# An operand shifted by 32 bytes and five steps reordered in a fused convolution and two-layer kernel

## The chip, the core and the metric

The kernel runs on one core of a Trainium2 chip. The metric is the device time of one execution in microseconds (us). A profile records one execution, instruction by instruction, on the engines PE (matrix products; its weight loads are listed as PEld), DVE (vector), ACT (activations, copies), POOL (a second elementwise engine, which also issues some DMAs) and SP (issues most of the DMAs).

## The reference

The input x has 8 sequences of 4096 tokens with 192 channels. A causal convolution of 7 taps per channel (the weights are a softmax over the taps, one set for each of 8 heads) gives y. Two dense layers follow:

```python
y   = sum over k of w[head, k] * x_padded[:, t + k, :]      # (8, 4096, 192)
h   = y.reshape(32768, 192) @ w_in                           # 192 -> 2048
g   = h * clip(h + 3, 0, 6) / 6
out = g @ w_out                                              # 2048 -> 192, float32
```

## The kernel before

The tokens are worked off in 32 blocks of 1024. Block 0 is a special case (its convolution, the rounding of the weights and a plain second layer stand there together). Blocks 1 to 31 each run `first_layer` (lines 457 to 515) and `second_layer` (lines 548 to 812).

**Convolution.** The tile `x` holds the 192 channels as 64 partitions times 3 thirds, with the lower 512 tokens of the block in partitions 0 to 63 and the upper 512 in partitions 64 to 127. `conv_jobs` (line 922) returns seven jobs that build the tile `y`: one ACT multiplication (tap 0, line 924) and six DVE operations (taps 1 to 6, line 926, one instruction each). There is one buffer for `x`: the load of the next but one block (`load_x`, lines 88 and 89, two DMAs on SP's queue) cannot start until tap 6 has read the old one. The loop at lines 1023 to 1038 spreads the jobs: taps 0, 1 and 2 of block i+2 stand in the list `between` of `second_layer(i)`, taps 3 to 6 in the list `jobs` of the following first layer, where key -1 is ahead of the first unit and key n is behind unit n.

**Splitting.** y is split for a product in several passes: `split_high` (ACT, line 420) writes a high part, `split_rest` (DVE, line 423) the low part, both into `y_own`, two tiles of the pool `yo`. `swap_parts` (line 427) copies both parts with the two halves of the partitions exchanged into `y_other`, by four DMAs of SP's queue (lines 299 and 300).

**First layer.** Sixteen units; units 0 to 7 read `y_own` and units 8 to 15 read `y_other`. A unit is 18 matmuls of 64 rows (line 437, three passes by three thirds by two partition halves, the two halves side by side in the array), then `relu` on ACT (line 311) and `gate` on DVE (line 315), which writes g. A unit holds two PSUM banks, one of four slots; the slot is free again after its gate. The last slots of the first layer are the first ones of the second layer.

**Second layer.** g is used as a two by two matrix of blocks A11, A21, A12, A22, and multiplied by w_out in seven products with sums of the blocks: S1 = A21 + A22 (written over A21), S2 = S1 - A11 (over A11), S3 = A11 - A21 in the tile `s3`, later S3 holds S4 = A12 - S2. Products 1, 4 and 5 are cut once more in the same way into seven small ones; their sums are `s1` (POOL, line 534), `s5` (DVE, line 534) and, for A22, the tile `z` and two tiles z2 and z4. z2 and z4 are called `z_early` and lie in the same memory as `y_own`, which is free by then. They are made by ACT (`seed`, line 477) and then by adding DMAs on POOL's queue (`onto`, line 480), in this order: two into `z`, one into the lower half of S1 (line 511), one into z2 (line 512), and one into z4 out of z2 (line 515).

The products of the second layer stand in four streams, one for each 32 columns of the PE array. Every instruction has a due time t in steps of one matmul of 256 columns; `put` appends matmuls, `do(t, ...)` puts a step of another engine at t - 0.5, and lines 806 to 808 emit everything sorted by t. The due time only sets the order in which each engine meets its instructions; when one runs is up to the semaphores. In the later part of the layer stand, by due time, S4's first half (line 760, DVE), `split_rest` (57.3), `swap_parts` (58), tap 0 (60), the add that the code builds for step 3 of product 5 (line 721, reads the bank slice B; due 61), U3's add (line 762, reads the bank `b` between products 6 and 3, due 61), S4's second half (line 763) and the stores.

Two bookkeeping tiles matter for addresses only: `mx` (line 257) and `sm` (line 264), each one float per partition.

Of the kernel before, what the change touches and what calls it, by code (L numbers as in the profile page):

```python
# [11 lines left out]
F32 = mybir.dt.float32  # L12
# [19 lines left out]
def kernel(  # L32
# [9 lines left out]
    P = nc.NUM_PARTITIONS  # L42
# [24 lines left out]
    cst = ctx.enter_context(tc.tile_pool(name="cst", bufs=1))  # L67
    xs = ctx.enter_context(tc.tile_pool(name="xs", bufs=1))
    ys = ctx.enter_context(tc.tile_pool(name="ys", bufs=1))
    yo = ctx.enter_context(tc.tile_pool(name="yo", bufs=1))  # L70
    ot = ctx.enter_context(tc.tile_pool(name="ot", bufs=1))
# [11 lines left out]
    def load_x(i, dma=nc.sync):  # L83
        x = xs.tile([P, K3, PAD + N], F32, name="x")
        head, lower, upper = x_source(i)
        if head:
            nc.vector.memset(x[0:D2, :, 0:PAD], 0.0)
        dma.dma_start(out=x[0:D2, :, head:], in_=lower)
        dma.dma_start(out=x[D2:P, :, :], in_=upper)
        return x  # L90
# [23 lines left out]
    make_identity(nc, ident[:])  # L114
    diag = cnv.tile([P, KC, P], F32, name="diag", bufs=1)
    g = cst.tile([P, NP, 2, G, N], F32, name="g")
    zeros = g[:, 0, 0, 0]
    nc.vector.memset(zeros, 0.0)

# [2 lines left out]
    def own_tiles(name):  # L122
        return [yo.tile([P, K3, N], F32, name=f"{name}{n}", tag=f"y{n}") for n in range(2)]

    y_own, z_early = own_tiles("y"), []
    y_other = cst.tile([P, 2, K3, N], F32, name="y_other")
    w_out = cst.tile([P, NP, 7, DH], F32, name="w_out")
# [126 lines left out]
        if n == 0:  # L254
            load_x0(1, nc.sync, nc.sync)

    mx = cst.tile([P, 1], F32, name="mx")
    nc.vector.tensor_reduce(out=mx[:], in_=w_sb[:], axis=AX.X, op=ALU.max)
    e_sb = cst.tile([P, KC], F32, name="e_sb")
    nc.vector.tensor_tensor(  # L260
        out=e_sb[:], in0=w_sb[:], in1=mx[:].to_broadcast([P, KC]), op=ALU.subtract
    )
    nc.scalar.activation(e_sb[:], e_sb[:], ACT.Exp)
    sm = cst.tile([P, 1], F32, name="sm")
    c_sb = cst.tile([P, KC], F32, name="c_sb")
    half = cst.tile([P, 1], F32, name="half")
    nc.vector.memset(half[:], 0.5)
# [42 lines left out]
    def relu(r6, h):  # L310
        nc.scalar.activation(r6, h, ACT.Relu, bias=half[:], scale=1.0 / 6.0)  # L311

    def gate(g_, h):

        nc.vector.scalar_tensor_tensor(  # L315
            out=g_, in0=g_, scalar=1.0, in1=h, op0=ALU.min, op1=ALU.mult
        )
# [57 lines left out]
    def g_sums(engine, which, slots, width):  # L375

        forms = {
            3: (S3, A11, A21, ALU.subtract),
            2: (S2, S1, A11, ALU.subtract), 4: (S3, A12, S2, ALU.subtract),
        }  # L380
        for n in which:
            o, a, b, op = forms[n]
            for p in slots[::width]:
                r = slice(p, p + width)
                engine.tensor_tensor(out=o[:, r], in0=a[:, r], in1=b[:, r], op=op)  # L385
# [18 lines left out]
    def add(out, x, y, op=ALU.add):  # L404
        nc.vector.tensor_tensor(out=out, in0=x, in1=y, op=op)  # L405
# [9 lines left out]
    m = slice(0, DH)  # L415
# [15 lines left out]
    def products(n, slot, s, steps=range(3), begin=False, end=False):  # L431
        group, c = divmod(n, NP)
        for m_ in steps:
            wn, yn = PASSES[m_]
            for k in range(2):
                r = slice(k * D2, (k + 1) * D2)
                nc.tensor.matmul(  # L437
                    out=psum[:, 2 * slot + k], lhsT=r32(w_in_parts[wn][r, c, s]),
                    rhs=r32(y_other[r, yn, s] if group else y_own[yn][r, s]),
                    start=begin and m_ == 0, stop=end and m_ == 2, skip_group_check=True,  # L440
                )

    def places(n, slot):
        group, c = divmod(n, NP)
        return g4[:, c, 1:3] if group else g4[:, c, 0::3], psum[:, 2 * slot : 2 * slot + 2]


    def sums_a22():

        z2, z4 = (  # L450
            part[:].rearrange("p s n -> p (s n)")[:, : NP * TH // 2]
            .rearrange("p (u t) -> p u t", t=TH)
            for part in z_early
        )
        return z[:, :, 1], z2, z[:, :, 0], z4

    def first_layer(i, jobs):

        def unit(n):
            slot = free_slots.pop(0)  # L460
            for m_ in range(3):
                for s in range(K3):
                    products(n, slot, s, (m_,), s == 0, s == K3 - 1)
            to, both = places(n, slot)
            relu(to, both)
            gate(to, both)
            free_slots.append(slot)

        count = 2 * NP
        x11, x12, x21, x22 = four_parts(A22)  # L470

        def begin_sums():
            z_early[:] = own_tiles("z")
            seed(sums_a22()[1], x11, -1.0)

        def seed(to, x, sign):
            nc.scalar.mul(to, x, sign)  # L477

        def onto(to, x):
            nc.gpsimd.dma_start(out=to, in_=x, accum_op=ALU.add)  # L480


        def z13(u0, u1):
            onto(z[:, u0:u1].rearrange("p u c t -> p (u c) t"), A22[:, 2 * u0 : 2 * u1, halves[1]])

        hu = NP // 4
        s4_sums = {
            hu + 1: [lambda: seed(z[:, :hu, 0], x11[:, :hu], -1.0)],
            hu + 2: [lambda: seed(z[:, :hu, 1], x21[:, :hu], 1.0), lambda: z13(0, hu)],
            NP - 1: [lambda: seed(z[:, hu:, 0], x11[:, hu:], -1.0)],  # L490
            NP: [lambda: seed(z[:, hu:, 1], x21[:, hu:], 1.0), lambda: z13(hu, 2 * hu)],
            NP + 1: [begin_sums],
            NP + 2: [lambda: seed(sums_a22()[3], x12, -1.0)],
        }
        for job in jobs.get(-1, ()):
            job()
        for n in range(count):
            unit(n)
            for job in jobs.get(n, ()):
                job()  # L500
            for job in s4_sums.get(n, ()):
                job()
            if n == 1:
                s1.append(ot.tile([P, NP, N], F32, name="s1", tag="shared")[:])
            if n < NP and n % 2:
                small_sums(s1[-1], A11, (1, 2, 3, 4), nc.gpsimd, every[n - 1 : n + 1])
            if n > NP and n % 2:
                pair = slice(n - NP - 1, n - NP + 1)
                g_sums(nc.gpsimd if n + 1 < count else nc.vector, (3,), range(NP)[pair], 2)
                if n == NP + 3:  # L510
                    onto(S1[:, : NP // 2], A22[:, : NP // 2])
                    onto(sums_a22()[1], z[:, :, 1])
        for pair in (slice(NP - 2, NP), slice(NP - 4, NP - 2)):
            add(S1[:, pair], A21[:, pair], A22[:, pair])
        onto(sums_a22()[3], sums_a22()[1])
# [4 lines left out]
    def four_parts(x):  # L520
        return [x[:, c::2, t] for t in halves for c in range(2)]

    def small_sums(to, x, which, engine=nc.gpsimd, r=every):

        r = slice(r[0], r[-1] + 1)
        x11, x12, x21, x22 = four_parts(x[:, r])
        s1, s2, s3, s4 = four_parts(to[:, r])
        forms = {
            1: (s1, x21, x22, ALU.add), 2: (s2, s1, x11, ALU.subtract),
            3: (s3, x11, x21, ALU.subtract), 4: (s4, x12, s2, ALU.subtract),  # L530
        }
        for n in which:
            o, p, q, op = forms[n]
            engine.tensor_tensor(out=o, in0=p, in1=q, op=op)  # L534
# [13 lines left out]
    def second_layer(i, between):  # L548
        last = i + 1 == NB
        ours = [free_slots.pop(0) for _ in range(3)]  # L550
        d, e, b, c, a, x_ = (psum[:, 2 * n + k] for n in ours for k in range(2))
# [3 lines left out]
        m = slice(0, DH)  # L555
# [3 lines left out]
        late = {}  # L559
# [8 lines left out]
        def do(t, fn, *args, **kw):  # L568
            streams[3].append((t - 0.5, lambda: fn(*args, **kw)))  # L569
# [189 lines left out]
        do(44, sum_s5, 4)  # L759
        do(44, g_sums, nc.vector, (4,), every[:4], 4)  # L760
        do(53, lambda: copy(out=late["p7"], in_=c[m]))
        do(61, lambda: add(late["u3"], b[m], late["p7"]))
        do(61, g_sums, nc.vector, (4,), every[4:], 4)
        do(65.5, lambda: add(late["p7"], late["u3"], p4[:]))
        do(65.5, lambda: store(i, late["p7"], 1, 0))
# [69 lines left out]
    with tc.manual_schedule():  # L835
# [19 lines left out]
        b, b1 = (2 * free_slots[-1] + k for k in range(2))  # L855
# [81 lines left out]
        for r in range(2 * NP):  # L937
# [12 lines left out]
            n = joins.get(r)  # L950
# [42 lines left out]
        conv = []  # L993
# [27 lines left out]
        z = last.tile([P, NP // 2, 2, TH], F32, name="z")  # L1021
        left = []
        for i in range(1, NB):
            jobs = {4 * n + 1: [job] for n, job in enumerate(conv[4:])}
            jobs[-1] = left + conv[3:4]
            first_layer(i, jobs)
            conv = []

            def begin_conv():
                x_tiles[i + 2] = load_x(i + 2)  # L1030
                conv.extend(conv_jobs(i + 2))

            between = []
            if i + 1 < NB:
                between = [(43.6, split_high), (57.3, split_rest), (58, swap_parts)]
            if i + 2 < NB:
                between += [(20, begin_conv), (60, lambda: conv[0]()), (72, lambda: conv[1]()), (73, lambda: conv[2]())]
            left = second_layer(i, between)


# [31 lines left out]
```

## Time and profile before

| what | value |
|---|---|
| time, median of 3 runs | 2243.15 us (2242.98 to 2243.4) |
| the profiled execution | 2243.17 us, span 2241.4 us |
| PE busy | 2227.6 us (99% of the span) |
| DVE, ACT, POOL busy | 1833.1, 1163.6, 900.7 us |
| one first layer (144 matmuls on y_own, 144 on y_other) | about 33.3 us |
| one second layer | 35.36 us in nearly every other block, mostly 35.7 to 36.4 us in those between |
| DMA traffic | 208.1 MB, of which 98.7 MB on POOL's queue |

In the page's groups a line gives line, engine, operation, tiles, partitions by elements and count, then busy time and mean ns of one, then the idle time of the engine ahead of them. Matmuls of line 437 overlap in pairs, so that the time from start to start says more than the mean of one. In a timeline the first column is the start from the beginning of the span, the second the length, and in brackets stands how long the engine had been idle and for what.

### The profile page before, as it was taken

The numbers are of one execution on the slowest core, as the hardware profiler recorded it, in microseconds if no ns is written. First come the engines' busy times: TensorE is split into PE (matmuls) and PEld (weight loads), VectorE is DVE, ScalarE is ACT, GpSimd is POOL, SyncE is SP. The second block draws the span as 40 slices with busy tenths as digits, with TensorE's granted clock in tenths as the row PEclk, the third lists the DMA queues.
The fourth block names the chain that finished last, engine by engine and source line by source line (L and its number), as shares of the span: only waits on it lengthen the run. The fifth ranks groups of instructions, "written<-read, shape, count | busy, mean of one in ns | idle before, by whom it ended". The sixth has DMA issues, their size and how long they took to land.

```text
span 2241.4 us, 51884 instructions
## 1 busy us (share of the span) xinstructions
PE 2227.6 (99%) x22466; PEld 1531.3 (68%) x22466; DVE 1833.1 (82%) x1650; ACT 1163.6 (52%) x1607; POOL 900.7 (40%) x803
## 2 busy tenths in 40 slices
PE   9999999999999999999999999999999999999998
PEld 5567676677666676766767667676667676676766
DVE  8887888878888778887788887788877888878876
ACT  7455554455554555544555445555455554555544
POOL 4534442244432444323444224443244432344423
PEclk9999999999999999999999999999999999999999
DMA  7355544555545545445554455554554544555353
GB/s 163 67 106 91 100 84 83 105 96 89 97 73 102 105 83 103 80 87 107 93 97 83 86 105 94 92 94 74 104 103 83 104 74 93 107 85 99 71 90 63
DMA packets 302181, 208.10 MB, mean 93 GB/s; under 512 B 208608, under 2 KB 261344, under 8 KB 301952
## 3 DMA queue, kind: packets, MB, share of 16 engines
q0 software_dynamic: 70320, 98.65, 28.0%
q1 hardware_dynamic: 230392, 105.86, 22.9%
q8 instruction: 176, 2.88, 0.6%
q10 hardware_dynamic: 1240, 0.27, 0.1%
q14 instruction: 53, 0.43, 0.1%
HBM read 31.72 MB, written 25.17 MB: 25 GB/s over the span
## 4 chain that ended last, share of the span: by engine, by line
PE 83%; DVE 10%; DMA 6%; POOL 1%; issue 0%; ACT 0%; SPq 0%; DVEq 0%; POOLq 0%; ACTq 0%
PE psum L437 45%; PE psum L572 35%; DMA z<-z 5%; DVE s L385 3%; DVE y L423 2%; DVE results L405 2%; PE psum L326 2%; DVE z L405 2%; POOL s L534 1%; PE psum L850 0%; POOL s L385 0%; DVE y L926 0%; DMA w_sb<-in_weight_dram 0%; DMA y_other<-y 0%; POOL z L480 0%
## 5 line engine op out<-in xcount | busy, mean ns | idle before, releaser
L572 PE MATMUL psum<-g,w_out 128*32 128x512 f32 (+1 forms) x6092 | 1051.2, 531 | 0.0
L315 DVE SCALAR_TENSOR_TENSOR g<-g,psum 128x1024 f32<-128x1024 f32 x512 | 618.9, 1218 | 192.5 <-ACT g L311 190.0
L311 ACT ACTIVATE g<-psum,half 128x1024 f32<-128x1024 f32 x512 | 571.4, 1116 | 355.0 <-PE psum L437 350.4
L534 POOL TENSOR_TENSOR s<-g 128x256 f32<-128x256 f32 x248 | 251.6, 1014 | 1005.4 <-DVE g L315 972.2
L572 PE MATMUL psum<-s,w_out 128*32 128x256 f32 (+1 forms) x3272 | 628.9, 571 | 2.9
L437 PE MATMUL psum<-y,w_in 64*128 64x512 f32 x4608 | 548.9, 393 | 0.3
L437 PE MATMUL psum<-y_other,w_in 64*128 64x512 f32 x4608 | 530.1, 386 | 0.1
L572 PEld LDWEIGHTS psum<-g,w_out 128*32 128x32 f32 x6092 | 421.7, 110 | 146.9 <-issue 44.0
L437 PEld LDWEIGHTS psum<-y,w_in 64*128 64x128 f32 x4608 | 428.0, 184 | 135.5 <-issue 26.7
L437 PEld LDWEIGHTS psum<-y_other,w_in 64*128 64x128 f32 x4608 | 431.7, 184 | 92.7 <-DMA y_other<-y 0.5
L926 DVE SCALAR_TENSOR_TENSOR y<-x,c_sb,y 128x1536 f32<-128x1536 f32 x186 | 336.7, 1810 | 2.9 <-ACT y L924 1.8
L572 PE MATMUL psum<-g,w_s 128*32 128x256 f32 x1488 | 322.3, 379 | 0.0
L385 POOL TENSOR_TENSOR s<-g 128x1024 f32<-128x1024 f32 x93 | 301.1, 3238 | 6.5 <-DVE g L315 6.5
L572 PEld LDWEIGHTS psum<-s,w_out 128*32 128x32 f32 x3272 | 180.4, 110 | 168.6 <-issue 116.7
L534 DVE TENSOR_TENSOR g<-g 128x1024 f32<-128x1024 f32 x93 | 111.2, 1224 | 121.6 <-PE psum L572 121.6
L572 PE MATMUL psum<-z,w_s 128*32 128x256 f32 x992 | 201.8, 380 | 2.4 <-DMA z<-z 2.0
L572 PEld LDWEIGHTS psum<-g,w_s 128*32 128x32 f32 x1488 | 156.7, 110 | 39.8
L385 DVE TENSOR_TENSOR s<-g 128x2048 f32<-128x2048 f32 (+1 forms) x93 | 179.4, 1929 | 1.1
L480 POOL DMA_DIRECT2D z<-z x62 | 83.4, 1345 | 233.5 <-ACT psum L718 81.0
L572 PE MATMUL psum<-s,w_s 128*32 128x256 f32 x744 | 170.7, 379 | 0.0
L569 ACT COPY psum<-psum 32x512 f32<-32x512 f32 (+1 forms) x217 | 106.3, 490 | 106.9 <-PE psum L572 103.1
L477 ACT ACTIVATE z<-g 128x512 f32<-128x512 f32 x186 | 143.2, 770 | 30.5 <-DVE g L315 30.4
(97 smaller groups left out, 1697.0 us busy)
## 6 DMA issues: line engine op xcount, KB each, us to landing
y_other<-y SPq DMA_DIRECT2D x124, 384.0 KB, 5.0
z<-g POOLq DMA_DIRECT2D x62, 512.0 KB, 5.7
g<-g POOLq DMA_DIRECT2D x31, 1024.0 KB, 8.2
z<-z POOLq DMA_DIRECT2D x62, 512.0 KB, 8.3
out_dram<-results SPq DMA_DIRECT2D x378, 64.0 KB, 2.0
x<-in_x_dram SPq DMA_DIRECT2D x53, 388.5 KB, 6.4
g<-in_moe_w_in_dram SPq DMA_DIRECT2D x16, 192.0 KB, 5.6
stage<-in_moe_w_out_dram SPq DMA_DIRECT2D x8, 384.0 KB, 5.3
```

The lines of the kernel that those rows point to most:

```text
L311: nc.scalar.activation(r6, h, ACT.Relu, bias=half[:], scale=1.0 / 6.0)
L315: nc.vector.scalar_tensor_tensor(out=g_, in0=g_, scalar=1.0, in1=h, op0=ALU.min, op1=ALU.mult)
L326: lambda p=p: nc.tensor.matmul(out=bank[j * QS : (j + 1) * QS, tokens], lhsT=w_out[:, p, w, cols], rhs=x[:, p, tokens], start=(first and p ...
L385: engine.tensor_tensor(out=o[:, r], in0=a[:, r], in1=b[:, r], op=op)
L405: nc.vector.tensor_tensor(out=out, in0=x, in1=y, op=op)
L437: nc.tensor.matmul(out=psum[:, 2 * slot + k], lhsT=r32(w_in_parts[wn][r, c, s]), rhs=r32(y_other[r, yn, s] if group else y_own[yn][r, s]), ...
L477: nc.scalar.mul(to, x, sign)
L480: nc.gpsimd.dma_start(out=to, in_=x, accum_op=ALU.add)
L534: engine.tensor_tensor(out=o, in0=p, in1=q, op=op)
L569: streams[3].append((t - 0.5, lambda: fn(*args, **kw)))
L572: nc.tensor.matmul(out=out, lhsT=w, rhs=x, start=start, stop=True, tile_position=(0, j * QS), skip_group_check=True,)
L926: jobs.append(lambda k=k: nc.vector.scalar_tensor_tensor(out=y[:], in0=x[:, :, k : k + N], scalar=c_sb[:, k : k + 1], in1=y[:], op0=ALU.mu ...
```

## The change

- `sm` becomes a tile of the pool `yo`, allocated ahead of `y_own`, and `mx` a tile of the pool `ot`. Every tile takes a multiple of 32 bytes of each partition. So the tiles behind them in memory move by 32 or 64 bytes: the two tiles that hold `y_own` (and later z2 and z4) move from byte 171968 and 178112, both multiples of 64, to 171936 and 178080, both 32 past a multiple of 64. `y_other` (118944) and the three w_in tiles (82080, 94368, 106656) lie 32 past a multiple of 64 before and after; `y` stays on a multiple of 64, the tiles `s`, `results`, `z`, `p1`, `p4` do not move.
- The DMA that adds `z[:, :, 1]` into z2 is issued ahead of the one that adds A22 into the lower half of S1.
- U3's add is due at 60.9 instead of 61. It then stands ahead of the add that reads B on DVE.
- `split_rest`, `swap_parts` and tap 0 are due at 62, 63 and 64 instead of 57.3, 58 and 60. On DVE the low part is now behind S4's second half. On ACT and on SP no instruction changes place.
- Tap 2 leaves the second layer. In the first layers of blocks 2 to 30 the taps 2 to 6 now stand ahead of unit 0 and behind units 1, 5, 9 and 13; before, the taps 3 to 6 stood ahead of unit 0 and behind units 1, 5 and 9. Block 1 keeps its old places.

```diff
+    mx = ot.tile([P, 1], F32, name="mx")
...
+    sm = yo.tile([P, 1], F32, name="sm")
     y_own, z_early = own_tiles("y"), []
...
-    mx = cst.tile([P, 1], F32, name="mx")
...
-    sm = cst.tile([P, 1], F32, name="sm")
...
                 if n == NP + 3:
+                    onto(sums_a22()[1], z[:, :, 1])
                     onto(S1[:, : NP // 2], A22[:, : NP // 2])
-                    onto(sums_a22()[1], z[:, :, 1])
...
-        do(61, lambda: add(late["u3"], b[m], late["p7"]))
+        do(60.9, lambda: add(late["u3"], b[m], late["p7"]))
         do(61, g_sums, nc.vector, (4,), every[4:], 4)
...
-            jobs = {4 * n + 1: [job] for n, job in enumerate(conv[4:])}
-            jobs[-1] = left + conv[3:4]
+            rest = conv[2 if i > 1 else 3 :]
+            jobs = {4 * n + 1: [job] for n, job in enumerate(rest[1:])}
+            jobs[-1] = left + rest[:1]
...
-                between = [(43.6, split_high), (57.3, split_rest), (58, swap_parts)]
+                between = [(43.6, split_high), (62, split_rest), (63, swap_parts)]
...
-                between += [(20, begin_conv), (60, lambda: conv[0]()), (72, lambda: conv[1]()), (73, lambda: conv[2]())]
+                between += [(20, begin_conv), (64, lambda: conv[0]()), (72, lambda: conv[1]())]
```

## The prediction

> **What bounds the kernel now.** I read the page's busy times first, then its groups:
>
> ```profile
> PE 2227.6 (99%) x22466; PEld 1531.3 (68%) x22466; DVE 1833.1 (82%) x1650; ACT 1163.6 (52%) x1607; POOL 900.7 (40%) x803
> ...
> L437 PE MATMUL psum<-y,w_in 64*128 64x512 f32 x4608 | 548.9, 393 | 0.3
> L437 PE MATMUL psum<-y_other,w_in 64*128 64x512 f32 x4608 | 530.1, 386 | 0.1
> ```
>
> PE is the bound. Only what shortens its stream or fills its gaps counts. The two groups of line 437 do equal work and differ: 393 against 386 ns. PE's timeline of the first layer of one block shows the same from start to start:
>
> ```profile
> 1061.02 17.06 PE L437 MATMUL psum<-y,w_in 64*128 64x512 f32 x144
> 1077.92 16.52 PE L437 MATMUL psum<-y_other,w_in 64*128 64x512 f32 x144
> 1094.37 0.62 PE L572 MATMUL psum<-g,w_out 128*32 128x512 f32 x1
> ```
>
> 16.90 us on `y_own`, 16.45 us on `y_other`. Inside the halves a pair of matmuls starts every 233.3 and every 226.7 ns, evenly. In block 0, where units of the two kinds alternate every 2 us, the slow pace goes with the `y_own` units and runs on for some five pairs, so it belongs to the operand and not to what else runs.
>
> Next, who waited for whom, for PE's weight loads:
>
> ```profile
> PEld psum L572 <- DVE results L405: 26.3, 60, 0.6
> ...
> PEld psum L572 <- DMA z<-z: 9.8, 19, 1.0
> ```
>
> The first is U3's add: two columns wait in each of 30 blocks, 0.44 us. The second is the add into z2, in every other block. Then the timelines of DVE, POOL, SP and PE around one second layer (it starts at 1094.37):
>
> ```profile
> 1091.55 1.22 DVE L315 SCALAR_TENSOR_TENSOR g<-g,psum 128x1024 f32<-128x1024 f32 x1 [0.82 <-ACT g L311]
> 1093.59 1.22 DVE L315 SCALAR_TENSOR_TENSOR g<-g,psum 128x1024 f32<-128x1024 f32 x1 [0.82 <-ACT g L311]
> ...
> 1101.08 2.36 DVE L534 TENSOR_TENSOR g<-g 128x1024 f32<-128x1024 f32 x2 [0.58 <-PE psum L572]
> 1106.62 1.23 DVE L534 TENSOR_TENSOR g<-g 128x1024 f32<-128x1024 f32 x1 [3.17 <-PE psum L572]
> 1107.88 0.43 DVE L405 TENSOR_TENSOR p<-psum,p 32x256 f32<-32x256 f32 x1
> ...
> 1119.73 1.76 DVE L423 TENSOR_TENSOR y<-y,y 128x1536 fp32r<-128x1536 f32 x1
> 1121.52 1.14 DVE L405 TENSOR_TENSOR results<-psum,results 32x256 f32<-32x256 f32 x2
> ```
> ```profile
> 1091.48 1.31 POOL L480 DMA_DIRECT2D g<-g  x1 [0.30 <-POOL s L385]
> 1092.27 1.84 POOL L480 DMA_DIRECT2D z<-z  x1
> ```
> ```profile
> 1086.40 0.58 SPq L88 DMA_DIRECT2D x<-in_x_dram  x1
> ```
>
> The gates 13 and 14; the sums that read S1 and the add behind them; the low part of y ahead of B's and U3's adds; the adds into S1 and z2; and x's load, which starts as soon as tap 6 (behind unit 9) has let go of the buffer. Last, the DMA rates, in windows that hold x's load, then S1's add, and of two queues at once (block 0's end):
>
> ```profile
> 1089.20:1092.20 3.00, 3.00 (x30) 2.49 (x28) 1.87 (x2) 1.40 (x2) 2.70 (x2) 1.00 1.01 231
> 1093.50:1098.50 5.00, 5.00 (x58) 2.40 (x58) 4.03 (x4) 2.06 (x4) 3.03 (x2) 1.00 1.10 186
> ```
> ```profile
> 83.20:84.20 1.00, 1.00 (x16) 0.29 (x12) 0.97 (x2) 0.00 (x0) 1.00 (x2) 1.00 1.10 190
> ```
>
> The last two columns are the busy share of the DMA engines and GB/s: one transfer alone fills them.
>
> **The parts.** The profiled execution took 2243.17 us (2241.4 span, 1.8 around it), the median 2243.15, so the sum starts at 2243.2.
>
> *Address of `y_own`.* No row shows it at another address. `y_other` and the weights lie 32 past a multiple of 64, `y_own` on one; afterwards all agree. Upper bound: `y_own` takes `y_other`'s pace, 72 pairs x 6.6 ns = 0.475 us a block; with five pairs after the change of operand 0.49; 31 blocks 15.3 us, block 0 some 0.6. Lower bound: nothing, as line 572 runs the same steps on `s` (multiple of 64) as on g (32 past): one product of 512 columns every 858 ns in both. A loss of the same size stays possible. I take -15.4: the nearest rows are those of the same line and form. z2 and z4 move too, but are read by line 572: 0. The Trainium skill, "TensorE: Matmul & The Clock Gate", section "Back-to-back issue gap", gives a gap of N / 2.4 + 2.5 ns, 215.7 for 512, with no address in it; by that this part would be 0 and the sum 2240.2. The trace disagrees, with 233.3 and 226.7.
>
> *U3's add ahead.* DVE takes the low part at 1119.73 and so reaches U3's add at 1121.95; it ends at 1122.64 and PE goes on at 1122.72, 0.40 late, with 0.02 of restart. Bank `b` is complete at about 1121.1 (last matmul of product 6 starts at 1120.07, a pass takes 0.86). Moved, U3's add runs 1121.12 to 1121.81, and PE needs it at 1122.32: 0.5 to spare. 30 blocks x 0.43 = -12.9. Next late: S4's second half, then 1122.2 to 1124.5, needed at 1125.8. B's add feeds only the stores.
>
> *The low part, swaps, tap 0.* The low part ends at 1126.1 instead of 1121.5. SP's two last swap DMAs wait for it; behind them stand only stores, whose data come later still. `y_other` is due some 20 us later. On ACT tap 0 now waits until 1126.1, with step 4's copy (1123.17 before) and the copy of line 805 behind it; their bank slices are next written in units 2 and 3 of the new first layer, after 1133. Nothing; were that cover gone, 1.6 us for tap 0.
>
> *Tap 2 leaves.* DVE's chain at the change of block has one tap (1.75 us) less but starts 1.3 later: the gates of the first units come 0.1 earlier against PE. Nothing.
>
> *A tap behind unit 13.* It is queued ahead of gate 14. Gate 13 ends at 1092.77, the tap costs 1.73 (start to next start of the one behind unit 9), so gate 14 runs 1094.50 to 1095.72 instead of 1093.59 to 1094.81. Its bank is first overwritten at 1095.70; with 0.06 for the semaphore a stall of 0.08, by contention with POOL up to 0.2. Gate 15 is late by 0.1, with 1.7 us to spare. 29 blocks x 0.1 = +2.9.
>
> *z2's add first.* It takes S1's place in POOL's queue; what it waits for (the second add into `z`) has landed by 1089.5. It lands near 1097.2 instead of 1102.6; PE needs it at 1103.46. The 16 late second layers are 0.08 to 1.05 longer than 35.36 us; in sum 10.3, by the waits 9.8. I take -10. z4's add waits for z2 and then queues behind S1's; due at 1111.
>
> *S1's add second, and against x's load.* This is the unknown. With tap 6 behind unit 13, x's load is issued not at 1086.40 but near 1094.6 and flows from 1096.7, inside S1's add. Alone, S1's add would land where z2's does now, 8.4 to 8.5 into the layer. The load holds 0.79 MB at 231 GB/s: 3.4 us. If the engines share fully and gain nothing, S1 lands at 11.9. If two queues hide each other, at 8.5. The window of two queues has the same busy share as one alone (1.10) and moves 190 GB/s, where its two transfers alone do 239 and 121 (80.5 to 83.0 and 86.2 to 88.5), mean 180: sharing with a small gain. That window reads HBM in its one transfer as x's load does, so I stay nearer to full sharing and take two thirds, 2.2: 10.7. Further, an instruction fetch (176 packets of 16 KB, 1.0 to 1.4 us of one engine each) falls into this stretch in most blocks and holds up one engine's part: 11.6 in those. The cost: the sums at 1101.08 wait for S1, then 2.3 for the two, 1.26 for the third, 0.43 for the add, 0.1 of semaphores, 4.1 in sum; PE overwrites what that add reads at 1109.07, 14.7 into the layer. So PE stalls for landing minus 10.6: 0.1 or 1.0. Half of each: 0.6 in the 28 blocks with both the moved tap and a load (2 to 29), +17. Ends: 0 and, with 11.9 and a fetch in each (12.9), 2.3 a block, +64. The Trainium skill, "DMA: Bandwidth & Descriptors", section "Queues, rings and completion order", says that an engine goes round-robin between the queues that it has work for, which by itself makes full sharing and the slower rival below; the shared window agrees in kind.
>
> Sum: 2243.2 - 15.4 - 12.9 - 10 + 2.9 + 17 = 2224.8.
>
> **Rivals.**
> - *S1 in time.* The load hides in S1's add, or the fetches miss it. For it: the sums have 3.17 us of idle behind them. Against: busy shares above 1 for one queue alone. 2224.8 - 17 = 2208.
> - *Slower: S1's add pays for all of x's load.* Landing at 11.9, 12.9 where a fetch hits. Half of each is a stall of 1.8 in 28 blocks, +50: 2258. It decides from a mean stall of 1.26 us, a landing of 11.9, where it eats the other 35.4. For it: the shares above 1.
> - *The address does nothing.* The pace hangs on something else that tells the two tiles apart (distance to the weights, larger powers of two). 2224.8 + 15.4 = 2240, no change. For it: line 572's indifference. Against: both parts of `y_other`, 6144 bytes apart, keep the fast pace. The Trainium skill's gap (above) would side with this rival.
>
> **The numbers.** Chances: the sum as it stands 0.48; S1 in time 0.20; slower 0.17; no effect of the address 0.12; other mixes 0.03. 0.2% is 4.5 us, about what a measurement of this kernel can tell. Faster: 0.46 of the first, all of the second, a third of the fourth, 0.70. Slower: 0.16 of the third and 0.04 of the rest, 0.20. Same: 0.10. The range 2204 to 2250 takes in S1 in time and a stall of up to 1.5 us; the likeliest's own range is 2213 to 2240.
>
> **What would show it.** Line 437's two groups at the same mean ns, halves of 16.4 each; the wait on DVE results of line 405 gone where the low part stood; no wait on z<-z; a second layer of 34.9 us plus a new wait of PE or its loads near 14.7 us into it, put down to DVE's adds into p, with the DVE sums of line 534 released by g<-g; gate 14 about 0.9 later. Wrong it would be if `y_own` kept 393 ns, or if that new wait exceeded 1.26 us a block.

## The result, and the profile after

The changed kernel takes 2235.11 us (median of 6 runs, 2233.61 to 2237.25) against 2243.15 for the kernel before (6 runs, 2242.96 to 2243.59): 0.9964 of it, with a 95% interval of 0.9951 to 0.9977. That is 8.0 us faster, where the prediction had 18.4. The profiled execution took 2235.09 us, its span is 2233.3, and the clock was granted in full.

The page of the changed kernel, its busy times and the two groups of the first layer's matmuls (line numbers are one higher than before):

```profile
PE 2222.2 (100%) x22466; PEld 1519.3 (68%) x22466; DVE 1828.4 (82%) x1650; ACT 1159.6 (52%) x1607; POOL 893.9 (40%) x803
...
L438 PE MATMUL psum<-y,w_in 64*128 64x512 f32 x4608 | 534.9, 388 | 0.3
L438 PE MATMUL psum<-y_other,w_in 64*128 64x512 f32 x4608 | 529.0, 386 | 0.1
```

The two groups now agree within 2 ns. PE's timeline of the same first layer that the prediction showed says it from start to start:

```profile
1056.58 16.61 PE L438 MATMUL psum<-y,w_in 64*128 64x512 f32 x144
1073.03 16.48 PE L438 MATMUL psum<-y_other,w_in 64*128 64x512 f32 x144
1089.44 0.62 PE L573 MATMUL psum<-g,w_out 128*32 128x512 f32 x1
```

Both halves take 16.4 us; a pair of matmuls starts every 226.7 ns in each. Over the run the first layers went from 33.34 to 32.87 us on average, 14.6 us in 31 layers, and block 1 starts 0.2 us earlier.

The waits (engine, line, what it waited for, total us, times, longest):

```profile
DVE g L535 <- DMA g<-g: 113.3, 24, 5.8
...
PEld psum L573 <- DVE p L406: 23.4, 28, 1.6
...
PEld psum L573 <- DVE g L316: 8.9, 29, 0.3
```

The waits on U3's add and on z2 are gone. In their place PE's weight loads wait in 28 layers, those with x's load beside them, for an add into p1, and ahead of it DVE's sums wait for S1's adding DMA. The timelines of DVE, POOL, SP and the weight loads around the second layer that starts at about 1089.5:

```profile
1087.76 1.81 DVE L927 SCALAR_TENSOR_TENSOR y<-x,c_sb,y 128x1536 f32<-128x1536 f32 x1
1089.49 2.43 DVE L316 SCALAR_TENSOR_TENSOR g<-g,psum 128x1024 f32<-128x1024 f32 x2
...
1101.27 3.50 DVE L535 TENSOR_TENSOR g<-g 128x1024 f32<-128x1024 f32 x3 [5.68 <-DMA g<-g]
1104.79 0.96 DVE L406 TENSOR_TENSOR p<-psum,p 32x256 f32<-32x256 f32 x2
```
```profile
1086.56 1.29 POOL L481 DMA_DIRECT2D z<-z  x1
1087.35 1.82 POOL L481 DMA_DIRECT2D g<-g  x1
```
```profile
1089.64 0.58 SPq L88 DMA_DIRECT2D x<-in_x_dram  x1
```
```profile
1103.69 0.11 PEld L573 LDWEIGHTS psum<-g,w_out 128*32 128x32 f32 x1
1105.27 0.11 PEld L573 LDWEIGHTS psum<-g,w_s 128*32 128x32 f32 x1 [1.47 <-DVE p L406]
```

S1's add is issued at 1087.35. x's load is issued 2.3 us later, from SP, as soon as the tap at 1087.76 has let go of the buffer. The sums get S1 at 1101.27, and the weight load comes 1.47 late.

A second layer's length, from its first matmul to the first of the next block, splits the 8 us. It was 35.36 us undisturbed, 35.70 on average. Now it is 35.04 in blocks 1 and 30, which have no load beside S1's add, and 36.00 on average in the 28 others (35.51 to 36.75). So, against before:

| where | us |
|---|---|
| first layers, 31 x 0.47 | -14.6 |
| block 0, up to the start of block 1 | -0.2 |
| undisturbed second layer 0.31 shorter, 30 times | -9.4 |
| z2's lateness in the second layers, gone | -10.3 |
| the new stall, 28 x 0.957 | +26.8 |
| from the second layer of block 31 to the end | -0.3 |
| sum | -8.0 |

In each of the 28 layers the length is the start of DVE's sums after the layer's start, plus 24.90 to 24.92 us. (The start of the sums is counted here and below at the small semaphore instruction ahead of them on DVE, 0.10 us before the first sum itself: 11.73 and 11.83 in the layer shown.) Sums that start at 10.14 or earlier therefore cost nothing. They start at 10.60 to 11.84, on average 11.10; in blocks 1 and 30 at 8.03 and 8.11.

### The profile page after: what moved, and what is told of

It is laid out like the page before. It is cut to its first block, busy times and chain, and to the rows that moved or that the text cites. A ratio compares the mean times of both kernels' runs of the same rounds, so it can differ in the third digit from the quotient of the medians.

```text
span 2233.3 us, 51856 instructions
## 1 busy us (share of the span) xinstructions
PE 2222.2 (100%) x22466; PEld 1519.3 (68%) x22466; DVE 1828.4 (82%) x1650; ACT 1159.6 (52%) x1607; POOL 893.9 (40%) x803
## 4 chain that ended last, share of the span: by engine, by line
PE 92%; DVE 2%; POOL 2%; DMA 2%; issue 1%; ACT 1%; SPq 0%; DVEq 0%; POOLq 0%; ACTq 0%
PE psum L573 47%; PE psum L438 44%; PE psum L327 2%; DMA g<-g 1%; POOL s L535 1%; DMA out_dram<-results 0%; DVE g L535 0%; POOL s L386 0%; DVE s L386 0%; POOL z L481 0%; DVE p L406 0%; DMA x<-in_x_dram 0%; DVE results L406 0%; SPq L353 0%; DVE g L316 0%
## 5 line engine op out<-in xcount | busy, mean ns | idle before, releaser
L535 POOL TENSOR_TENSOR s<-g 128x256 f32<-128x256 f32 x248 | 245.2, 989 | 1214.4 <-DVE g L316 928.0
L438 PE MATMUL psum<-y,w_in 64*128 64x512 f32 x4608 | 534.9, 388 | 0.3
L573 PEld LDWEIGHTS psum<-g,w_out 128*32 128x32 f32 x6092 | 385.6, 109 | 168.6 <-issue 47.2
L573 PE MATMUL psum<-g,w_s 128*32 128x256 f32 x1488 | 327.7, 379 | 3.2 <-DVE p L406 2.9
L573 PEld LDWEIGHTS psum<-s,w_out 128*32 128x32 f32 x3272 | 223.9, 110 | 103.8 <-issue 69.3
L573 PE MATMUL psum<-z,w_s 128*32 128x256 f32 x992 | 206.3, 380 | 0.0
L925 ACT ACTIVATE y<-x,c_sb 128x1536 f32<-128x1536 f32 x31 | 48.9, 1578 | 211.3 <-issue 211.3
```

The source lines that it names most:

```text
L438: nc.tensor.matmul(out=psum[:, 2 * slot + k], lhsT=r32(w_in_parts[wn][r, c, s]), rhs=r32(y_other[r, yn, s] if group else y_own[yn][r, s]), ...
L573: nc.tensor.matmul(out=out, lhsT=w, rhs=x, start=start, stop=True, tile_position=(0, j * QS), skip_group_check=True,)
L925: jobs = [lambda: nc.scalar.mul(y[:], x[:, :, 0:N], c_sb[:, 0:1])]
```

## The experiments

Twelve kernels were run, each beside the kernel before. The theory after the result: each part did what its row in the table says, and the 26.8 come from x's load running beside S1's add.

### The address alone

```diff
-    mx = cst.tile([P, 1], F32, name="mx")
+    mx = ot.tile([P, 1], F32, name="mx")
...
-    sm = cst.tile([P, 1], F32, name="sm")
+    sm = yo.tile([P, 1], F32, name="sm")    # ahead of y_own
```

> The kernel before with only the two one-float tiles moved, so that y_own starts 32 bytes past a multiple of 64. If the address alone sets the pace of the first layer: the own half falls from 16.90 to 16.46 us in each of the 31 first layers, the other half stays at 16.41 to 16.44, the second layers stay as before, and the time falls by 31 x 0.47 + 0.5 = 15.1 to about 2228. If the first layers became shorter because of the other edits (the moved taps, the later split), nothing changes: 2243.

Measured: 2227.9 us (0.9933, 0.9919 to 0.9948). Own halves 16.46, other halves 16.41, second layers 35.69 on average as before. The address is worth 15.0 us by itself.

### The address of the weights

```diff
+    mx = cst.tile([P, 1], F32, name="mx")    # taken from further back
     w_in_parts = [cst.tile([P, NP, K3, P], F32, name=f"w_in{n}") for n in range(3)]
...
+    sm = cst.tile([P, 1], F32, name="sm")    # taken from further back
     y_other = cst.tile([P, 2, K3, N], F32, name="y_other")
```

> The kernel before with the three w_in tiles moved from 32 past a multiple of 64 to a multiple of 64; y_own stays on a multiple of 64, y_other 32 past one. If the moving operand's own address counts: own half 16.90, other half 16.44, as before, 2243. If moving operand and weights must agree modulo 64: the halves change places, own 16.44 and other 16.90, time again about 2243. If the weights' address counts for itself: both halves change by the same amount, +15 (both 16.9 or slower) or -15.

Measured: 2240.49 us (0.9988, 0.9979 to 0.9998). The two groups on its page:

```profile
L439 PE MATMUL psum<-y_other,w_in 64*128 64x512 f32 x4608 | 544.5, 392 | 0.1
L439 PE MATMUL psum<-y,w_in 64*128 64x512 f32 x4608 | 534.8, 388 | 0.3
```

The halves have changed places: own 16.46 us, other 16.90, a pair every 226.7 and every 233.3 ns. `y_own` has not moved; `y_other` is where it was modulo 64. So it is not the moving operand's own address that counts, but whether moving operand and weights lie alike modulo 64. (The tiles that agree modulo 64 in these runs agree modulo 256 too, and those that do not are 32 apart, so whether 64 or a larger power of two is what counts is not shown.) The 2.4 us less than before lie in the second layers, 2.0 of them (the waits on z2 were shorter); why is open.

### The order of the adding DMAs alone

```diff
+                    onto(sums_a22()[1], z[:, :, 1])
                     onto(S1[:, : NP // 2], A22[:, : NP // 2])
-                    onto(sums_a22()[1], z[:, :, 1])
```

> The kernel before with only the order of the two adding DMAs changed; x's load still runs before the second layer. If S1's add is late in the changed kernel because of the load beside it: here it lands about 8.1 us into the layer, before the 10.1 that the sums may wait, no new stall, and the waits on z2 go: second layers of 35.36 all alike, -10.3, 2232.9. If the order alone makes S1 too late: sums start at 10.5 or later, a new wait of about 0.9 in most layers, 2243 or more.

Measured: 2232.57 us (0.9954, 0.9939 to 0.9969), second layers of 35.354 to 35.356 without exception. Of its waits, the one for S1:

```profile
DVE g L534 <- DMA g<-g: 81.1, 29, 3.9
```

The sums do wait for S1, but start at 8.95 on average and 9.99 at the latest, below 10.14. No wait on z2 and none on p is left. The order is worth 10.4 us as long as nothing runs beside it. The sums start a microsecond later in the even blocks, at 9.46 against 8.45 in the odd ones. The even blocks are those in which a 16 KB instruction fetch starts 7 to 8 us into the layer, while S1's add moves. The odd blocks from 3 to 13 have no fetch inside it and start at 8.02 to 8.21; those from 15 on have one at 2.2 to 2.4 us and start at 8.67 to 8.86. That the fetch is the cause was not tested, and blocks 26 and 28, with the fetch at 7.8 to 7.9, start at only 8.35 and 8.44.

### U3's add and the later low part alone

```diff
-        do(61, lambda: add(late["u3"], b[m], late["p7"]))
+        do(60.9, lambda: add(late["u3"], b[m], late["p7"]))
...
-  (57.3, split_rest), (58, swap_parts)  ...  (60, lambda: conv[0]())
+  (62, split_rest), (63, swap_parts)    ...  (64, lambda: conv[0]())
```

> The kernel before with U3's add due at 60.9 and the low part, the swaps and tap 0 due at 62, 63 and 64. By the prediction's term the wait of 0.43 in each of 30 second layers goes: -12.9, 2230.3. By the second layers of the changed kernel that have no load beside them (35.04 us against 35.36): 0.32 a layer, -9.5, 2233.6.

Measured: 2247.36 us (1.002, 1.0011 to 1.003), slower than before; both expectations miss. The second layers that wait for nothing take 35.04, so 0.32 a layer is right where nothing else ends last. But its waits show what took it back:

```profile
PEld psum L572 <- DMA z<-z: 16.9, 26, 1.4
...
PEld psum L437 <- DVE g L315: 9.0, 29, 0.4
```

The wait of line 437 is new: with the low part later and tap 2 still in the second layer, DVE comes to the first gates of the next block too late, and the own half grows from 16.90 to 17.03, 3.9 us in all. Everything behind it on DVE and POOL is later too: x's load is issued at -7.36 us from the second layer's start instead of -7.96, the last adding DMA ahead of the layer at -1.43 instead of -1.93, and the weight loads' waits on z2 are 26 with 16.9 us instead of 19 with 9.8. The second layers gain 0.6 us in all instead of 9.5.

### U3's add behind B's again

```diff
-        do(60.9, lambda: add(late["u3"], b[m], late["p7"]))
+        do(61, lambda: add(late["u3"], b[m], late["p7"]))
```

> The changed kernel with U3's add due at 61 again, so that on DVE it stands behind the add that reads B; the low part stays behind S4's second half. In the undisturbed second layers of the changed kernel U3's add runs from 26.54 to 27.23 us, the weight load that waits for it is at 27.53 and its matmul at 27.95. If B's add (0.43) is then run first and the wait hangs on the weight load: U3's add ends at 27.70, a wait of about 0.15 to 0.2 in 30 layers, +4 to +6. If the wait hangs on the matmul's own start, or B's add finds an idle DVE before U3's input is there: nothing, 2235. If the step from 61 to 60.9 carried the gain of 0.32 a layer by itself: +9.5, 2244.6.

Measured: 2239.71 us (0.9985, 0.9976 to 0.9994). In blocks 1 and 30 the layer takes 35.04 as with the step: U3's add ends 0.47 later (at 27.70 instead of 27.23), its weight load comes 0.23 later (27.76), the matmul still starts at 27.95. So the step from 61 to 60.9 adds nothing once the low part has moved; the low part's move is enough for the whole gain. The 4.6 us more lie in the 28 layers: the sums that wait for S1 start at 11.25 on average instead of 11.10, which makes 4.4 by the relation above. S1's add is issued 0.13 us later on average (at -2.16 instead of -2.29), which is most of the 0.16; why it is issued later is open. U3's step to 60.9 without the low part's move was not run.

### The old places of the taps in the changed kernel

```diff
-            rest = conv[2 if i > 1 else 3 :]
-            jobs = {4 * n + 1: [job] for n, job in enumerate(rest[1:])}
-            jobs[-1] = left + rest[:1]
+            jobs = {4 * n + 1: [job] for n, job in enumerate(conv[4:])}
+            jobs[-1] = left + conv[3:4]
...
+  (73, lambda: conv[2]())    # tap 2 in the second layer
```

> The changed kernel with tap 2 back in the second layer and taps 3 to 6 back ahead of unit 0 and behind units 1, 5 and 9, so that x's load starts some 8 us before the second layer. If the load beside S1's add is the whole of the new stall (28 layers, 0.96 us each): all second layers 35.04 us, 2235.1 - 26.8 = 2208.3. If the new order of the adds makes the stall, the load or not: 2235.

Measured: 2222.15 us (0.9907, 0.9889 to 0.9924), half of the expected gain. The waits on its trace:

```profile
PEld psum L438 <- DVE g L316: 7.2, 15, 0.5
...
PEld psum L573 <- DVE p L406: 6.6, 14, 0.7
```

14 second layers still stall, 7.9 us in all, and the first layers are 5.9 us longer. As with U3's add and the low part alone, DVE is late at the change of block. x's load is out of S1's way here: it is issued at -7.17, and its last data packet ends at 0.3 us on average, while the first packet of S1's add starts at 3.15, so that no packet of the load moves beside it. What makes S1 late is its own issue: at -1.02 on average instead of -2.44 with the order alone, its first packet 1.43 us later. The sums start at 10.7 in the even blocks and 9.5 in the odd ones, where the order alone had 9.46 and 8.45. So the expectation lacked a third case, an add that is late with no load beside it. The run puts all the taps back at once, so it does not tell tap 2's place from that of the others; what it shows is that the later low part is free only with the new places.

### x's load behind the adds, on POOL's queue

```diff
-                x_tiles[i + 2] = load_x(i + 2)
+                x_tiles[i + 2] = load_x(i + 2, nc.gpsimd)
```

> The changed kernel with x's load issued on POOL's queue, behind S1's and z4's adds, instead of SP's; the tap behind unit 13 stays. If the sharing of the DMA engines between the two queues makes S1 late: the sums start about 8.1 us into the layer in all blocks, no wait near 14.1, 2208. If the moved tap itself (gate 14 later, S1's input later) makes it late: the sums stay at 10.6 to 11.8, 2235.

Measured: 2212.02 us (0.9863, 0.9847 to 0.9878). 27 of the 28 layers take 35.04; the sums start at 9.23 on average. Only the load's place was changed, the tap stays behind unit 13: the load beside S1's add is the cause of the stall, and the moved tap is not. The first layers are 2.8 us longer than in the changed kernel (the own half waits for gates in 10 blocks). The expected 8.1 for all blocks was missed, but not because of the load: its first packet starts at 10.46 us at the earliest, after S1 has landed in every block. With the order alone, too, the sums start at 8.95 on average; here S1's first packet starts 0.27 us later than there (1.99 against 1.72), and the sums 0.28.

### S1 first, with the late load

```diff
-                    onto(sums_a22()[1], z[:, :, 1])
                     onto(S1[:, : NP // 2], A22[:, : NP // 2])
+                    onto(sums_a22()[1], z[:, :, 1])
```

> The changed kernel with the two adds in the order of before (S1, then z2); x's load still late. By the sharing account S1 is now in time (about 6.5 us into the layer), and z2 pays for the load: it lands at about 11 instead of 8.2, PE needs it at 9.1, a stall of about 2 us in 28 layers: 2208 + 56 = 2264. If the load only gets what the adds leave over, z2 waits as before (10 us in all) and the time is about 2218.

Measured: 2313.97 us (1.0319, 1.0302 to 1.0335), a stall of 3.7 us a layer instead of 2. In one layer, from 195.59, the weight load that needs z2 and POOL's issue of z4's add, which reads z2:

```profile
207.83 0.13 PEld L573 LDWEIGHTS psum<-z,w_s 128*32 128x32 f32 x1 [3.05 <-DMA z<-z]
...
208.37 0.89 POOL L481 DMA_DIRECT2D z<-z  x1 [10.38 <-DMA z<-z]
```

z2 lands 12.2 us into the layer. The records of the DMA packets say why z2 gets less than S1 did. Counted over the 28 layers (averages for one layer, records of 4 bytes counted in), from 6.5 to 10 us, z2's add moved 316 packets and the load 310, almost the same number, but z2's packets hold 1 KB and the load's 2 KB: 92 GB/s for z2, 172 for the load. In the changed kernel, from 5 to 9 us, S1's add moved 257 packets and the load 259, both of 2 KB: 131 and 126 GB/s. So the two queues move nearly equal numbers of packets. The Trainium skill, "DMA: Bandwidth & Descriptors", section "Queues, rings and completion order", says that an engine goes round-robin between the queues at the granularity of packets; these counts agree, if each record that the profile calls a packet is a packet in that sense.

### x's load in smaller packets

```diff
-        dma.dma_start(out=x[0:D2, :, head:], in_=lower)
-        dma.dma_start(out=x[D2:P, :, :], in_=upper)
+        cuts = [0, N // 2, PAD + N] if i > 2 else [0, PAD + N]
+        for c0, c1 in zip(cuts, cuts[1:]):
+            h0 = max(c0, head)
+            dma.dma_start(out=x[0:D2, :, h0:c1], in_=lower[..., h0 - head : c1 - head])
+            dma.dma_start(out=x[D2:P, :, c0:c1], in_=upper[..., c0:c1])
```

> The changed kernel with x's load (blocks 3 to 31) cut into two DMAs for each half, so that its packets hold 1 KB instead of 2 KB; same bytes, same time of issue, same queue. If the DMA engines change between the two queues packet by packet: S1's add with its 2 KB packets then gets two thirds of the bytes instead of a half while both run; of the 0.76 MB that are left when the load's first packet comes at about 4.0, all have landed by 9, so the sums start before 10.13 in most layers and the stall (26.8) nearly goes: 2208 to 2214. If the engines share by bytes, or all goes as the load's length alone: sums at 10.6 to 11.8 as before, 2235.

Measured: 2214.63 us (0.9874, 0.986 to 0.9889). The wait:

```profile
PEld psum L576 <- DVE p L409: 2.6, 7, 0.6
```

From 5 to 8.5 us S1's add got 148 GB/s and the load 82, in 256 and 301 packets: near to equal numbers, though here the queue with the small packets moved more of them. The sums start at 10.20 on average, 0.9 earlier. The layers that stall are exactly those with a start of 10.16 or more (15 of them, 4.5 us in all); up to 10.06 none does. The four smaller DMAs also take SP longer to issue (4.8 us instead of 1.7), which spreads the load's second half; how much of the 0.9 that makes was not taken apart.

### The third sum behind p1's adds

```diff
-        for t, n in ((15.5, 1), (15.5, 3), (28.5, 2)):
+        for t, n in ((15.5, 1), (15.5, 3), (33.5, 2)):
```

> The changed kernel with the third of DVE's three sums that stand behind S1's add (1.22 us) put behind the two adds into p1. In the changed kernel the layer's length is the start of these sums plus 24.91 us in all 28 stalled blocks, so PE stalls from a start of 10.13 on. With 1.22 less ahead of the add that PE's weight load waits for, the bound moves to 11.35; with starts as in the changed kernel (10.60 to 11.84) only six layers still stall, by 1.7 us in all: 2235.1 - 26.8 + 1.7 = 2210. If PE needs what the sums write and not that add, nothing moves: 2235.

Measured: 2213.86 us (0.987, 0.9855 to 0.9886). The sums start 0.1 later than before the edit (11.21 on average), and yet the wait is nearly gone:

```profile
PEld psum L573 <- DVE p L406: 4.7, 23, 0.7
```

12 layers stall, by 3.1 us in all, and their length is the start of the sums plus 23.77: the bound has moved to 11.28, by the 1.13 to 1.15 that one sum less makes. PE needed the add into p1, not the sums ahead of it. The first layers are 1.8 us longer.

### Smaller packets and the third sum together

```diff
+        # x's load cut as above
...
-        for t, n in ((15.5, 1), (15.5, 3), (28.5, 2)):
+        for t, n in ((15.5, 1), (15.5, 3), (33.5, 2)):
```

> The cut load and the third sum behind p1's adds together. With the bound at 11.27 (the third sum behind the adds alone showed it) and sums that start at 9 to 10, all second layers take 35.04 us; what stays is what the first layers gave with the third sum moved alone (own half 0.06 longer, 1.8 in all): 2208.3 to 2211. If sharing goes by bytes: as with the third sum alone, 2214.

Measured: 2211.15 us (0.9858, 0.9841 to 0.9874), the fastest of all, 32 us below the kernel before and 24 below the changed one. Every second layer takes 35.04. The sums start at 9.82 to 10.88, later than the 9 to 10 of the expectation, but all before 11.28. The first layers are 3.1 us longer than in the changed kernel; no run shows how to get these back.

### Taps closer together

```diff
-            jobs = {4 * n + 1: [job] for n, job in enumerate(rest[1:])}
+            jobs = {3 * n + 1: [job] for n, job in enumerate(rest[1:])}
...
+        # and the third sum behind p1's adds
```

> The changed kernel with the third sum behind p1's adds, and taps 3 to 6 behind units 1, 4, 7 and 10 instead of 1, 5, 9 and 13, so that x's load is issued some 6 us earlier (about 6 us before the second layer) with tap 2 still outside the second layer. By the account: the load and S1's add overlap less, the sums start at 9.5 to 10.8 as with the old places of the taps, below 11.27: second layers of 35.04 throughout, 2208 to 2211. If the earlier taps make gates of the first layer late: own or other halves above 16.5, as much slower.

Measured: 2293.5 us (1.0224, 1.0208 to 1.0239), far from both expectations. The first layers are as in the changed kernel. But in 13 blocks the second layer takes 39 to 42 us, and PE waits for a POOL sum:

```profile
PEld psum L573 <- POOL s L386: 55.3, 13, 5.0
```

In 14 other blocks the old wait for the sums remains, 11.4 us in all. POOL's and SP's timelines ahead of one of the 13 layers, which starts at 264.23:

```profile
259.63 1.27 POOL L481 DMA_DIRECT2D z<-g  x1
260.43 5.26 POOL L386 TENSOR_TENSOR s<-g 128x1024 f32<-128x1024 f32 x2
268.96 1.29 POOL L481 DMA_DIRECT2D z<-z  x1 [3.26 <-PE psum L573]
269.75 1.80 POOL L481 DMA_DIRECT2D g<-g  x1
270.52 3.40 POOL L386 TENSOR_TENSOR s<-g 128x1024 f32<-128x1024 f32 x1
```
```profile
259.14 0.58 SPq L88 DMA_DIRECT2D x<-in_x_dram  x1
```

Now x's load meets the adding DMA before: the second add into `z`, issued at 259.63 behind it. That one lands at 268.4. z2's add, which reads `z`, waits for it in POOL's queue (the profile names PE, whose matmul had long been done), and behind it stand S1's add and the last sum into S3, which PE needs. But the load is only part of it. In the same block of the run with the third sum alone, the second add into `z` is issued 8.9 us ahead of the layer and lands 5.4 us later. Here it is issued 4.6 ahead and takes 8.8. So of the 7.7 us by which it lands later, 3.4 lie in its flight, beside the load, and 4.3 ahead of its issue, because POOL's small sums end that much later. Why these end late is open, and so is what the earlier load would cost with POOL on time.

## Why the prediction was right and wrong, step by step

The direction was right, and so was the order of size of the terms for the address, z2 and the stall; but the gain was 8.0 us instead of 18.4. Two terms were mis-sized: the cost of S1's add was taken 9.8 too small and U3's gain 3.5 too large. The 2.9 set down for gate 14, which cost nothing, made up for part of it.

| step | predicted | measured | shown by |
|---|---|---|---|
| address of `y_own` | -15.4 | -14.9 | the address alone: -15.0 |
| U3's add ahead | -12.9 | -9.4 | layers without another wait |
| low part, swaps, tap 0 later; tap 2 leaves | 0 | 0 together; +3.9 and more without tap 2's move | U3 and low part alone |
| a tap behind unit 13 | +2.9 | 0 | block 30; the load on POOL's queue |
| z2's add first | -10 | -10.3 | the order alone: -10.4 |
| S1's add against x's load | +17 | +26.8 | the load on POOL's queue; the third sum moved |

**The address.** The size was right to half a microsecond. (The prediction's own parts, 15.3 for 31 blocks and 0.6 for block 0, add up to 15.9, not to the 15.4 that it took.) Right was also the observation that operand and weights "afterwards all agree". Of what the prediction left open (own address, distance, or agreement) the moved weights decide for agreement: two tiles that had not changed modulo 64 changed places. The rival in which the address does nothing falls; its "larger powers of two" stay possible only as the period of the agreement. The gap that the Trainium skill's page "TensorE: Matmul & The Clock Gate" gives in its section "Back-to-back issue gap", 215.8 ns for 512 columns (the prediction has 215.7), is that of an isolated matmul and has no address in it; the runs show 226.7 and 233.3 for pairs of the same matmuls, by address alone.

**S1's add.** The step that failed is "PE stalls for landing minus 10.6". The landing was forecast at 10.7 or 11.6, on average 11.15, and the sums start at 11.10. But the bound is 10.14, not 10.6 (both counted at the start of the sums). It was worked out as 14.7, where PE overwrites what the add reads, less 4.1 for DVE's chain. The chain is 4.1: in the layer shown the sums take 3.5 and the first add half of the 0.96. The 14.7 was wrong: it is a later matmul of the same step. PE's weight loads and matmuls in the undisturbed layer of block 1, which starts at 127.64, have the load with this wait, its matmul and the matmul that the prediction took:

```profile
141.69 0.11 PEld L573 LDWEIGHTS psum<-g,w_s 128*32 128x32 f32 x1
```
```profile
141.91 0.38 PE L573 MATMUL psum<-g,w_s 128*32 128x256 f32 x1
...
142.34 0.38 PE L573 MATMUL psum<-g,w_s 128*32 128x256 f32 x1
```

They stand at 14.06, 14.27 and 14.70 us into the layer. 0.46 us too much slack in 28 layers is 13 us; the average of the stall was rounded up from 0.55 to 0.6, which gives part of it back.

That the landing came out right is partly luck. Its parts were wrong against each other. The order alone shows the start of the sums with no load beside S1's add: 9.46 in the even blocks, which have the fetch at 7 to 8 us, and 8.45 in the odd ones. In the changed kernel it is 11.03 and 11.16. So the load cost 1.6 us in the even blocks and 2.7 in the odd ones; 0.3 of the 2.7 is no sharing, since S1's first packet starts that much later there (2.04 against 1.71). The mean of 2.1 is close to the two thirds of 3.4 that the prediction took, but it hides two errors: the load takes more where no fetch falls, and the 0.9 that was added for the fetch does not show beside the load. Why the two delays do not add up is open. The slower rival's landing of 11.9 is 0.8 late on average; it needed a mean stall of 1.26, and 0.957 was reached.

**U3's add.** The wait was 0.43 in two columns, and without it three of the four streams of the PE array do run 0.43 earlier to the end of the layer. The layer ends 0.31 earlier. In the trace of before the fourth stream was already 0.12 behind the three (27.22 against 27.10 us into the layer), and the wait for U3's add held all four until they were level (28.36 to 28.37). Without it the lag stays to the end: the last matmuls start at 34.39 in the three streams and at 34.52 in the fourth, where before all started at 34.82 to 34.84. The wait had hidden a lag, and the term should have been sized by the stream that ends last. Who did it was misnamed, too: once the low part has moved, U3's place ahead of B's add gives nothing, since its weight load had that slack. Whether that place would have been enough by itself was not run.

**The low part later, tap 2 leaving.** "Nothing" for each is right only for the two together, and for the first layers (32.87 us, as with the address alone). The prediction looked for what waits behind the low part on SP and ACT, and missed DVE's own queue at the change of block, where the first gates of the next layer stand. Tap 2, 1.75 us, leaves just there; without that the own halves are 0.13 longer and x's load and the adds 0.5 to 0.6 later. S1's first packet starts 0.16 us later on average than with the order alone (1.88 against 1.72), which is part of the new stall; which of the moves makes that was not taken apart.

**Gate 14.** The trace has the forecast wait, 8.9 us in 29 layers, 0.3 each instead of 0.1. But block 30, which has the moved tap and no load, is as long as block 1, which has neither (35.04): the columns that waited make it good within the layer. A wait of one column near the start of a layer is not a term of the sum unless that column is the last at its end.

## What to carry to other kernels

Check where the moving operand and the weights of a matmul lie modulo 64: for the first layer's matmuls agreement is worth 2.9% of their pace, and moving two tiles of one float was enough. When a transfer is moved, name what it will run beside in its new place and compare packet sizes, since two queues here moved nearly equal numbers of packets: the add with the smaller packets lost most. And look at when it is issued: an add can be late with nothing beside it. Size a stall from the first instruction that carries the wait, and a gain from the column or chain that ends last, not from the wait that goes.

## What the runs showed of the hardware that was not expected

- An fp32r matmul of 512 columns on 64 rows starts every 226.7 ns (a pair) where operand and weights lie alike modulo 64, and every 233.3 ns where they differ by 32; which of the two lies on the multiple does not matter. Agreement modulo 64 without agreement modulo 256 was not run.
- Two queues that load the same DMA engines moved nearly equal numbers of packets, not of bytes: 257 to 259 with 2 KB each, 316 to 310 with 1 KB against 2 KB, 256 to 301 with 2 KB against 1 KB. Together they move some 257 GB/s with packets of 2 KB, where the load alone moved 231 and S1's add alone 186.
- A load queued behind the adding DMAs on the same queue moved no packet before S1's add had landed (10.46 us at the earliest, against landings at 8.2 to 10.3), and did not make that add later.
- Without a load beside it, S1's add landed a microsecond later in the blocks with a 16 KB instruction fetch 7 to 8 us into the layer (9.46 against 8.45 at the start of the sums); beside the load no such difference shows (11.03 against 11.16).
- A weight load ordinarily runs 0.2 to 0.4 us ahead of its matmul; one that came 0.23 late, 0.2 ahead of it, cost nothing.
